# Closing a decode kernel: the waits for the output DMAs move from the gathering of the engines to the reset of the semaphores, and the release of the engines goes

## The chip, the cores and the metric

The kernel runs on one core of one Trainium2 chip. The metric is the device time of one execution in microseconds (us). The profile tells engines apart as PE (matrix engine; PEld is its weight load), DVE (vector), ACT (scalar), POOL (GpSimd) and SP (sync); an engine name with a "q" behind it is that engine's sequencer, whose records below are waits, semaphore updates, drains and DMA issues. The span is the time from the first to the last instruction of the program in the profile; the measured time is longer (383.49 us against a span of 381.7 in before), and the trace records semaphore updates on both sides of the span, which are read here as runtime code.

A semaphore is a counter by which engines and DMAs signal each other; an update is one change of it, recorded in the trace with its time. The landing of a DMA is the last update of its semaphore. A drain is an instruction of the closing block that works on no tensor and can carry a wait or an update; an empty one carries neither. The gather is GpSimd's wait until all other engines have reported, the release its update that lets them go on. A hop is the time from one update of the runtime's barrier to the next.

A ratio given here is the mean time of one kernel's fast runs over that of the other's fast runs of the same rounds, so it is not quite the ratio of the medians quoted beside it. "Before" and "after" are the kernel without and with the change. Each set of experiments had its own runs of before on the same chip, and each time below is set against those.

## The reference, cut to what matters

```python
x = A_x                                             # one token, D = 1024
g = _sigmoid((x * gate_w).sum(-1, keepdims=True))
a = _A_ref(x, A_k_cache, A_v_cache, A_wq, A_wo)     # attention over 65536 cached keys, 4 KV heads of 128
b = _B_ref(x, B_w_in, B_w_sp, B_b_sp, B_w_out)      # a gated MLP
return g * a + (1 - g) * b                          # (1, 1, 1024), bf16
```

For one token, 162 MB of cache and weights are read, and 2 KB of result are written. The change does not touch any of this arithmetic.

## The kernel before

The end of the body, and the function that rewrites the program's closing block when the program is finalized:

```python
out_sb = const.tile([P, NO], BF16, name="out_sb")
nc.scalar.copy(out=out_sb[:], in_=out_ps[:])
for i, queue in enumerate((nc.scalar, nc.sync)):        # two output DMAs, from ACT and from SP
    p0 = (2 * i + 1) * B - 1
    ins = queue.dma_start(out=out_rows[2 * i:2 * i + 2, :], in_=out_sb[p0:p0 + 2, :])
    out_queues.append(ins.ins.name)
...
def close_with_one_barrier(n):
    block = n.main_func.blocks[-1]
    ...
        if engine == mybir.EngineType.Pool:
            assert kinds == ["InstDrain", "InstEventSemaphore", "InstEventSemaphore",
                             "InstDrain", "InstISA", "InstDrain", "InstEventSemaphore",
                             "InstEventSemaphore"]
            drop += [l[2][0], l[6][0]]
            closer = l[0][0]
            continue
        ...
        assert kinds == ["InstDrain", "InstEventSemaphore"] * 2
        drop += [l[1][0], l[2][0]]
    ...
    waits.sort(key=lambda w: w.id in final)             # the two output DMAs last
    block.instructions[closer] = copy.replace(
        block.instructions[closer], sync_info=mybir.SyncInfo(on_wait=waits, on_update=[]))
```

What remains in the closing block of before:

- PE, DVE, ACT and SP: a drain that adds 1 to the gather semaphore (number 96), then a wait for the release semaphore (97).
- GpSimd: waits for all loads and engines and, last, for the two output DMAs (semaphore 102 for the one from ACT, 103 for the one from SP); a drain; the gather (wait until 96 is 4); the reset drain; the clear of semaphores 99 to 110; a drain; the release (97 += 4).

Behind the last instruction of that block the trace of before still records nine updates of semaphore 2, which no instruction of the kernel names, one update each of 248 other semaphores (382.365 to 383.019 us), and nine more updates of semaphore 2. They are read here as closing code of the runtime: a barrier of all engines, a reset of the semaphores, and a second barrier.

## Time and profile before

| what | value | where it is read |
|---|---|---|
| time | 383.56 us median of 6 runs (383.31 to 383.75) | results |
| time and span of the profiled run | 383.49 and 381.7 us | results, head of the page |
| HBM loads | 98.7% of the span, 16 DMA engines | queues on the page |
| after the last load | 2.70 us with PE 0.28 and ACT 0.37 us busy | windows |
| later output landing to the end of the span | 381.698 - 381.028 = 0.670 us | records of the trace |
| first to last update of the runtime's first closing barrier | 382.456 - 381.937 = 0.519 us | updates of semaphore 2 |

The page of before. The DMA row is the busy share of the DMA engines in tenths, for 40 equal slices of the span; the queue's line has packets, MB and share:

```profile
span 381.7 us, 2586 instructions
...
DMA  9999999999999999999999999999999999999995
...
q1 hardware_dynamic: 4324, 162.01, 98.7%
```

Everything but the last slice is read as bound by the loads, whose packets fill 98.7% of the span. Next, busy time of each engine in two windows of before, with the granted clock, the share of DMA and GB/s at the end of each line:

```profile
345.00:379.00 34.00, 21.20 (x236) 8.66 (x182) 4.29 (x7) 0.00 (x0) 0.00 (x0) 0.80 0.95 402
379.00:381.70 2.70, 0.28 (x4) 0.08 (x3) 0.00 (x0) 0.37 (x1) 0.00 (x0) 1.00 0.00 1
```

In the last 2.70 us nothing is loaded (a DMA share of 0.00, 1 GB/s). The instructions of the closing block (all carry line 557) and the issue of the output DMAs (line 521) of before; columns are line, engine, operation, count, then the shortest, median and longest duration in ns, then the first and last start in us:

```profile
L521 SPq DMA_DIRECT2D out_dram<-out_sb x1: 315/315/315, 379.7 to 379.7; - x1
L521 ACTq DMA_DIRECT2D out_dram<-out_sb x1: 254/254/254, 379.7 to 379.7; - x1
...
L557 POOLq EVENT_SEMAPHORE  x7: 17/43/2600, 373.9 to 381.6; - x7
L557 POOLq DRAIN  x3: 34/41/72, 381.1 to 381.5; - x3
L557 DVEq DRAIN  x1: 343/343/343, 370.6 to 370.6; - x1
L557 PEldq DRAIN  x1: 345/345/345, 379.0 to 379.0; - x1
L557 ACTq DRAIN  x1: 241/241/241, 380.0 to 380.0; - x1
L557 SPq DRAIN  x1: 177/177/177, 380.1 to 380.1; - x1
L557 POOLq EVENT_SEMAPHORE_RANGE_CLEAR  x1: 96/96/96, 381.4 to 381.4; - x1
L557 SPq EVENT_SEMAPHORE  x1: 17/17/17, 381.6 to 381.6; - x1
L557 ACTq EVENT_SEMAPHORE  x1: 17/17/17, 381.6 to 381.6; - x1
L557 DVEq EVENT_SEMAPHORE  x1: 21/21/21, 381.6 to 381.6; - x1
L557 PEldq EVENT_SEMAPHORE  x1: 51/51/51, 381.6 to 381.6; - x1
```

The four engines had drained by about 380.3 us, but all three of GpSimd's drains start at 381.1 us or later: they stand behind the wait for the output DMAs. The same instructions with their full time stamps, and the updates of the semaphores, from the records of the trace of before (us from the span's start, duration in ns in brackets):

```
output DMAs issued     SP 379.721 [315]   ACT 379.725 [254]
landed in full         ACT (102) 380.853   SP (103) 381.028      <- the later one
GpSimd  wait 102+105 380.877 [43] | wait 103+107 381.052 [42] | drain 381.139 [41] | gather 381.224 [17]
        reset drain 381.304 [72] | clear 381.405 [96] | drain 381.530 [34] | release 381.594 [17]
others  take the release: SP 381.635  ACT 381.639  DVE 381.647  PE 381.647 [51], ends 381.698
semaphore 2, barrier just before the kernel: nine updates, -0.375 to -0.004
semaphore 2, first closing barrier:  381.937 381.971 382.172 382.216 382.239 382.337 382.375 382.409 382.456
semaphore 2, second closing barrier: 383.243 to 383.600
```

The start on record of a last wait is the moment it was met, not the moment it began: GpSimd's wait for semaphore 103 starts 24 ns after the landing's update in before (381.052 against 381.028).

### The profile page before, as it was taken

The page shows a single profiled execution, that of the slowest core. Times are in us where ns is not written, and L with a number is a line of the kernel's source. Part 1 is how long each engine was busy: PE and PEld are TensorE (multiplying, and loading weights), DVE is VectorE, ACT ScalarE, POOL GpSimd, SP SyncE. Part 2 cuts the span into 40 slices and gives each one's busy share as a digit, 9 for nine tenths or more (in the row PEclk, how much of TensorE's full clock was granted, in tenths as well). Part 3 has the DMA queues.
Part 4 walks back from the last instruction along what each step waited for, and adds up shares of the span by engine and source line. Part 5 has one row for each costly group of instructions (what it writes and reads, how often), then busy time and mean ns, then how long its engine had stood idle before and what let it go on. Part 6 is the DMA issues. An engine that isn't in the chain of part 4 may idle for free.

```text
span 381.7 us, 2586 instructions
## 1 busy us (share of the span) xinstructions
PE 229.4 (60%) x1372; PEld 56.6 (15%) x796; DVE 218.4 (57%) x211; ACT 39.6 (10%) x55; POOL 4.4 (1%) x10
## 2 busy tenths in 40 slices
PE   0433465678157934796379539762977196749355
PEld 0110011112011200121011101110111011212123
DVE  4241487996689306966996058669860497550040
ACT  1010001111601100114011001140100010500000
POOL 4000000000000000000000000000000000000000
PEclk9996569998669885989598958995889599969768
DMA  9999999999999999999999999999999999999995
GB/s 376 438 419 422 433 435 440 433 471 415 407 426 440 440 441 426 440 433 440 440 428 440 440 440 433 434 427 426 412 433 441 433 440 413 428 419 433 433 414 220
DMA packets 4376, 162.17 MB, mean 425 GB/s; under 512 B 521, under 2 KB 525, under 8 KB 909
## 3 DMA queue, kind: packets, MB, share of 16 engines
q1 hardware_dynamic: 4324, 162.01, 98.7%
q8 instruction: 8, 0.13, 0.1%
q14 instruction: 4, 0.02, 0.0%
q10 hardware_dynamic: 40, 0.01, 0.0%
HBM read 162.01 MB, written 0.00 MB: 424 GB/s over the span
## 4 chain that ended last, share of the span: by engine, by line
DMA 60%; PE 20%; DVE 15%; issue 1%; ACT 1%; SPq 1%; DVEq 0%; ACTq 0%
DMA kv<-in_A_k_cache_dram 38%; PE s_ps L388 15%; DVE kv L381 9%; DMA kv<-in_A_wo_dram 8%; DMA kv<-in_A_wq_dram 7%; DMA kv<-in_A_v_cache_dram 7%; PE o_ps L434 3%; DVE pt L424 2%; DVE mx L383 1%; DVE o_sb L448 1%; PE q_ps L274 1%; ACT sc L421 1%; DVE rowt L444 1%; ACT sc L399 1%; SPq L165 1%
## 5 line engine op out<-in xcount | busy, mean ns | idle before, releaser
L388 PE MATMUL s_ps<-kv,wt 128*128 128x512 bf16 x512 | 138.1, 427 | 85.4 <-DVE kv L381 85.4
L381 DVE STREAM_TRANSPOSE kv<-kv 128x2048 int32<-128x2048 int32 x64 | 142.7, 2280 | 58.8 <-DMA kv<-in_A_k_cache_dram 58.8
L434 PE MATMUL o_ps<-kv,pt 128*64 128x512 bf16 x512 | 62.6, 404 | 7.5 <-DMA kv<-in_A_v_cache_dram 7.5
L388 PEld LDWEIGHTS <-wt 128*128 128x128 bf16 x256 | 27.1, 106 | 197.7 <-issue 133.8
L399 ACT CAST sc<-s_ps 128x1024 bf16<-128x1024 f32 x16 | 16.2, 1013 | 253.0 <-PE s_ps L388 253.0
L434 PEld LDWEIGHTS <-pt 128*64 128x64 bf16 x256 | 16.2, 116 | 51.3 <-issue 48.4
L424 DVE STREAM_TRANSPOSE pt<-sc 128x1024 bf16<-128x1024 bf16 x16 | 18.6, 1217 | 6.8 <-ACT sc L421 6.8
L444 DVE TENSOR_TENSOR rowt<-o_ps,own 128x1024 f32<-128x1024 f32 x4 | 4.8, 1195 | 25.7 <-PE o_ps L434 25.7
L421 ACT ACTIVATE sc<-sc,nb 128x1024 bf16<-128x1024 bf16 x16 | 18.2, 1137 | 12.2 <-DVE nb L417 12.2
L383 DVE TENSOR_REDUCE mx<-sc 128x1 f32<-128x1024 bf16 x12 | 14.5, 1206 | 7.0 <-ACT sc L399 7.0
L454 PE MATMUL om_ps<-o_sb,hsel 128*32 128x128 f32 x8 | 2.5, 421 | 19.7 <-DVE o_sb L448 19.7
L403 DVE TENSOR_REDUCE mx<-sc 128x1 f32<-128x1024 bf16 x4 | 4.9, 1220 | 13.6 <-ACT sc L399 13.6
L274 PE MATMUL q_ps<-kv,xT 128*32 128x512 bf16 x64 | 7.2, 630 | 7.3 <-DMA kv<-in_A_wq_dram 7.3
L274 PE MATMUL z_ps<-kv,xT 128*32 128x448 bf16 x64 | 6.4, 577 | 3.9 <-DMA kv<-in_B_w_in_dram 3.9
L475 PE MATMUL out_ps<-kv,oa 128*32 128x256 bf16 x128 | 6.5, 364 | 3.3 <-DMA kv<-in_A_wo_dram 1.9
L341 DVE TENSOR_TENSOR rowt<-q_ps,own_b 128x512 f32<-128x512 f32 x2 | 1.3, 686 | 12.4 <-PE q_ps L274 12.4
L448 DVE TENSOR_REDUCE o_sb<-rowt 128x128 f32<-128x1024 f32 x4 | 7.5, 1872 | 0.1
L289 DVE TENSOR_TENSOR rowt<-z_ps,own_b 128x448 f32<-128x448 f32 x2 | 1.2, 620 | 8.6 <-PE z_ps L274 8.6
L274 PEld LDWEIGHTS <-xT 128*32 128x32 bf16 x64 | 3.0, 139 | 19.3 <-issue 19.3
L230 PE MATMUL xb_ps<-xg,spread 8*128 8x256 bf16 x1 | 0.4, 367 | 9.0 <-DMA xg<-in_gate_w_dram 9.0
L475 PEld LDWEIGHTS <-oa 128*32 128x32 bf16 x128 | 4.5, 129 | 5.5 <-issue 2.7
L518 ACT CAST out_sb<-out_ps 128x256 bf16<-128x256 f32 x1 | 0.4, 372 | 45.6 <-PE out_ps L475 45.6
(88 smaller groups left out, 54.9 us busy)
## 6 DMA issues: line engine op xcount, KB each, us to landing
kv<-in_A_k_cache_dram SPq DMA_DIRECT2D x4, 4096.0 KB, 26.8
kv<-in_A_wq_dram SPq DMA_DIRECT2D x2, 4096.0 KB, 32.9
kv<-in_A_v_cache_dram SPq DMA_DIRECT2D x2, 4096.0 KB
kv<-in_B_w_in_dram SPq DMA_DIRECT2D x2, 3584.0 KB, 15.1
kv<-in_A_wo_dram SPq DMA_DIRECT2D x1, 4096.0 KB
kv<-in_B_w_out_dram SPq DMA_DIRECT2D x1, 3584.0 KB
kv<-in_A_wo_dram SPq DMA_DIRECT2D x1, 2048.0 KB, 28.1
kv<-in_A_wo_dram SPq DMA_DIRECT2D x1, 1024.0 KB, 30.2
```

The source lines that it names most:

```text
L274: ins = nc.tensor.matmul(ps[t * B:(t + 1) * B, k * HN:k * HN + n], lhsT=xT[:, i * KH + c:i * KH + c + 1].to_broadcast([P, B]), rhs=w[:, c, ...
L381: nc.vector.transpose(out=kb[:, v * n:(v + 1) * n], in_=kb[:, v * n:(v + 1) * n])
L383: nc.vector.reduce_max(**late.pop())
L388: ins = nc.tensor.matmul(s_ps[:, k * HN:(k + 1) * HN], lhsT=wt[g % 2][:, v, b].rearrange("p a v h -> p (a v h)"), rhs=kx[:, b // 2, b % 2, ...
L399: nc.scalar.copy(out=sct[g, j][:], in_=s_ps[:])
L403: nc.vector.reduce_max(**late.pop())
L421: nc.scalar.activation(out=sct[g, j][:], in_=sct[g, j][:], func=ACT.Exp, scale=SCALE, bias=nb[:, 0:1], accum_out=lss[g][:, j:j + 1])
L424: nc.vector.transpose(out=ptt[g, j][:].rearrange("p c x -> p (c x)"), in_=sct[g, j][:])
L434: ins = nc.tensor.matmul(o_ps[g][hs, e, :], lhsT=ptt[g, j][:, 2 * u:2 * u + 2, :].rearrange("p c x -> p (c x)"), rhs=vx[:, 2 * u + e], sta ...
L444: nc.vector.tensor_tensor(out=om8, in0=o_ps[g][:].rearrange("p e (v d) -> p (e v) d", d=DH), in1=own_8[:].unsqueeze(2).to_broadcast([P, 2 ...
L448: nc.vector.tensor_reduce(out=o_sb[:], in_=om8.rearrange("p x d -> p d x"), axis=AX.X, op=ALU.add)
L475: nc.tensor.matmul(out_ps[t * B:(t + 1) * B, :], lhsT=vec[:, c0 + c:c0 + c + 1].to_broadcast([P, B]), rhs=w[:, c, t * NO:(t + 1) * NO], st ...
```

## The change

Its intent: GpSimd can do the drain and the gather while the output DMAs are still under way, and needs their completion only before it resets their semaphores. The other engines have nothing left to do once they have been gathered, so nobody needs to release them. The diff; every changed line is shown, "..." stands for unchanged ones:

```diff
-                drop += [l[2][0], l[6][0]]
-                closer = l[0][0]
+                drop += [l[2][0], l[6][0], l[7][0]]
+                closer, reset = l[0][0], l[3][0]
+                assert not l[3][2].has_wait() and not l[3][2].has_update()
                 continue
...
             assert kinds == ["InstDrain", "InstEventSemaphore"] * 2
-            drop += [l[1][0], l[2][0]]
+            drop += [l[1][0], l[2][0], l[3][0]]
...
-        waits.sort(key=lambda w: w.id in final)
-        block.instructions[closer] = copy.replace(
-            block.instructions[closer], sync_info=mybir.SyncInfo(on_wait=waits, on_update=[]))
+        for at, w in ((closer, [w for w in waits if w.id not in final]),
+                      (reset, [w for w in waits if w.id in final])):
+            block.instructions[at] = copy.replace(
+                block.instructions[at], sync_info=mybir.SyncInfo(on_wait=w, on_update=[]))
```

In the built program, the reset drain itself carries the wait for semaphore 102, and one more instruction ahead of it the wait for 103.

## The prediction

> **What bounds the kernel now.** The body is bound by HBM loads: on the page the DMA row is 9 tenths in all slices but the last, the load queue's packets fill 98.7% of the span, at 425 GB/s. The change touches only the last 2.7 us: in the window from 379.0 to 381.7 us the DMA share is 0.00, PE works 0.28 us and ACT 0.37 us. Everything there is serial and exposed.
>
> The closing instructions and the semaphore updates recorded in the trace give the end of before:
> - 379.695 the cast of the result ends; 379.72 both output DMAs are issued; ACT's has landed at 380.853, SP's at 381.028.
> - All four engines have reported to GpSimd by 380.272: the SP output DMA is the last thing awaited.
> - GpSimd after that: wait on SP's DMA 381.052, drain 381.139, gather 381.224, reset drain 381.304, range clear 381.405, drain 381.530 (34 ns), release 381.594 to 381.611. The four others take the release from 381.635; PE's is the last, 51 ns long, to 381.698.
>
> So 0.67 us lie between the last landing and the end of the span.
>
> **What changes, with costs.** No compute or load instruction moves on any engine.
> 1. The waits on the output DMAs move behind the gather, so the first drain and the gather run before the landing, near 380.3 us. From its wait (381.052) GpSimd goes to the reset drain in one step (about 87 ns): 381.304 - 381.139 = 0.165 us less, all on the critical path.
> 2. The release and the four waits for it go. The span then ends with GpSimd's last drain, which took to 381.564: 381.698 - 381.564 = 0.134 us less.
>
> The span should go from 381.70 to about 381.40 us.
>
> **From span to time.** The measured 383.49 is 1.8 us over the span of that run. In the trace the runtime's closing barrier follows: nine updates of semaphore 2 from 381.937 to 382.456, 0.52 us; the same nine took 0.37 us just before the kernel began and 0.36 us at the second closing barrier. [...] The extra is one hop of 0.201 us (381.971 to 382.172) in place of 0.038: one engine came late. If that is GpSimd, only its own earlier end counts: 381.611 to 381.40, -0.21 us. If it was an engine held by the release, up to about 0.16 us more can be gained. I expect -0.2 to -0.35 us, centre -0.25: 0.07%, below the spread of the three times before (383.31 to 383.65).
>
> **Prediction.** 383.25 us, 8 in 10 between 382.85 and 383.65. Faster by over 2%: 0.005; within 2%: 0.99; slower: 0.005.
>
> **What would show it.** Span about 381.4; gather and first drain of GpSimd near 380.3; reset drain about 0.1 us after the later landing; no instruction of PE, DVE, ACT or SP after about 380.3; the hop of 0.2 us gone or kept, which tells who was late; DMA share and groups unchanged.
>
> **What would make it wrong.** The output DMA's landing (1.3 us after its issue) varies by more than 0.2 us and hides or doubles the gain; the reset drain with a wait costs more than a plain one; the runtime's closing code waits for something later than GpSimd; run-to-run spread of the loads, some tenths, decides the sign of the medians.

0.165 and 0.134 us are read from the trace of before, and so are the hop of 0.201 us and the 0.038 us it is set against. The sums: -0.21 us if GpSimd is late, up to about 0.16 us more if another engine is, centre -0.25.

## The result, and the profile after

After takes 383.23 us (median of 6 runs, 383.11 to 383.30), before 383.56 us (6 runs). The ratio is 0.9992, 95% interval 0.9979 to 1.0005: "the same" at the level of per cents. The profiled runs of both, 383.12 and 383.49 us, are fast. The page and the windows of after:

```profile
span 381.3 us, 2581 instructions
...
q1 hardware_dynamic: 4324, 162.01, 98.8%
```

```profile
345.00:379.00 34.00, 19.33 (x224) 8.26 (x176) 4.29 (x7) 0.00 (x0) 0.00 (x0) 0.81 0.94 399
379.00:381.70 2.70, 0.18 (x4) 0.00 (x0) 0.00 (x0) 0.37 (x1) 0.00 (x0) 0.50 0.00 1
```

The loads are as they were. The fixed windows cut PE's work at slightly different places (236 against 224 matmuls recorded); in all, both pages count 1372 of PE. Five instructions are gone (2586 to 2581: the release and four waits for it). The closing block of after (its line is now 559, the output DMAs' 523), in the columns explained above:

```profile
L523 SPq DMA_DIRECT2D out_dram<-out_sb x1: 330/330/330, 379.6 to 379.6; - x1
L523 ACTq DMA_DIRECT2D out_dram<-out_sb x1: 258/258/258, 379.6 to 379.6; - x1
...
L559 POOLq EVENT_SEMAPHORE  x6: 17/43/10008, 368.8 to 380.9; - x6
L559 POOLq DRAIN  x3: 34/41/72, 379.7 to 381.2; - x3
L559 DVEq DRAIN  x1: 343/343/343, 369.1 to 369.1; - x1
L559 PEldq DRAIN  x1: 457/457/457, 378.8 to 378.8; - x1
L559 ACTq DRAIN  x1: 240/240/240, 379.9 to 379.9; - x1
L559 SPq DRAIN  x1: 164/164/164, 380.0 to 380.0; - x1
L559 POOLq EVENT_SEMAPHORE_RANGE_CLEAR  x1: 96/96/96, 381.1 to 381.1; - x1
```

GpSimd's first drain now starts at 379.7 us, 1.2 us ahead of the landing, and there is no line of SP, ACT, DVE or PE at the end. With full time stamps, from the records of the trace of after:

```
landed in full         ACT (102) 380.749   SP (103) 380.924
GpSimd  drain 379.680 [41] | gather 380.200 [17] | wait 103 380.948 [17]
        reset drain 381.009 [72] | clear 381.110 [96] | drain 381.235 [34], ends 381.269
semaphore 2, first closing barrier:  379.481 380.322 381.793 381.837 381.860 381.958 381.997 382.031 382.078
semaphore 2, second closing barrier: 382.865 to 383.223
```

The two profiled runs differ by 383.49 - 383.12 = 0.370 us. The trace splits that without a remainder:

| part | before | after | difference |
|---|---|---|---|
| span's start to the later landing (body and output DMA) | 381.028 | 380.924 | -0.104 |
| later landing to the third update of the first closing barrier | 1.144 | 0.869 | -0.275 |
| third update to the last update of the second barrier | 1.428 | 1.430 | +0.002 |
| last update to the measured time | -0.110 | -0.103 | +0.007 |
| sum | 383.490 | 383.120 | -0.370 |

The first row is the chance of the body: the cast of the result starts between 379.23 and 379.56 us in the fast profiles, and at 379.23 and 379.44 us in two profiles of one and the same kernel (after, and after again). The second row is the change. From here on that interval, later landing to third update, is what the experiments are judged by; the next section shows why the third.

### The profile page after: what moved, and what is told of

The parts are those of the page before. It is cut to its first block, busy times and chain, and to the rows that moved or that the text cites. A ratio compares the mean times of both kernels' runs of the same rounds, so it can differ in the third digit from the quotient of the medians.

```text
span 381.3 us, 2581 instructions
## 1 busy us (share of the span) xinstructions
PE 226.1 (59%) x1372; PEld 56.1 (15%) x796; DVE 218.5 (57%) x211; ACT 39.6 (10%) x55; POOL 4.4 (1%) x10
## 4 chain that ended last, share of the span: by engine, by line
DMA 60%; DVE 18%; PE 17%; issue 2%; ACT 1%; SPq 1%; DVEq 0%; ACTq 0%
DMA kv<-in_A_k_cache_dram 37%; PE s_ps L390 12%; DVE kv L383 12%; DMA kv<-in_A_wo_dram 9%; DMA kv<-in_A_wq_dram 7%; DMA kv<-in_A_v_cache_dram 7%; PE o_ps L436 3%; DVE pt L426 2%; DVE mx L385 1%; DVE o_sb L450 1%; PE q_ps L276 1%; ACT sc L423 1%; DVE rowt L446 1%; ACT sc L401 1%; SPq L167 1%
## 5 line engine op out<-in xcount | busy, mean ns | idle before, releaser
L436 PE MATMUL o_ps<-kv,pt 128*64 128x512 bf16 x512 | 60.4, 394 | 7.8 <-DMA kv<-in_A_v_cache_dram 7.8
```

Source lines behind the costliest of these rows:

```text
L436: ins = nc.tensor.matmul(o_ps[g][hs, e, :], lhsT=ptt[g, j][:, 2 * u:2 * u + 2, :].rearrange("p c x -> p (c x)"), rhs=vx[:, 2 * u + e], sta ...
```

## The experiments

Theory C: from the later landing on, one chain decides: GpSimd's remaining steps, then GpSimd's arrival in the runtime's barrier, then the barrier. Each step taken off GpSimd behind the landing counts in full; what the other engines do counts for nothing. Rival R: the engines that the release held back are what the barrier waits for, and freeing them is the gain. Rival D: the medians differ by drift of the loads. The kernels of all experiments gave the correct result.

### e1_late_wait: the first half alone

```diff
  (against after)
-                drop += [l[2][0], l[6][0], l[7][0]]
+                drop += [l[2][0], l[6][0]]
-            drop += [l[1][0], l[2][0], l[3][0]]
+            drop += [l[1][0], l[2][0]]
```

> Only the first half of the change: the output-DMA waits stand behind the gather, the release and the four waits for it stay. Theory C (chain through GpSimd): the drain and the gather leave the path after the later landing, so from that landing to the third update of the runtime's barrier it takes about 1.144 - 0.165 - 0.026 = 0.95 us (before 1.144, after 0.869); span about 0.19 us under before, time about 383.35 us. Theory R (rival: the other engines, held by the release, are what the runtime's barrier waits for, and freeing them is the gain): time stays within 0.05 us of before and the closing hop of 0.2 us stays because PE is still released last; landing to third update above 1.1 us. Theory D (rival: the medians differ by drift of the loads): any time, no relation to the closing.

Measured: 383.33 us (5 runs, 383.20 to 383.36) against 383.46 us for before (9 runs); ratio 0.9996, 0.9982 to 1.0010. Later landing (381.056) to third update (382.008): 0.952 us, 0.192 under before. The hop of 0.2 us is still there (381.807 to 382.008). Span end minus landing: 381.534 - 381.056 = 0.478 us, 0.192 under before's 0.670. So the first half gives 0.192 us by itself, with the release in place. The closing lines of e1:

```profile
L559 POOLq DRAIN  x3: 34/41/72, 379.8 to 381.4; - x3
...
L559 PEldq EVENT_SEMAPHORE  x1: 51/51/51, 381.5 to 381.5; - x1
```

GpSimd's first drain has moved ahead of the landing, and PE still takes the release last.

### e2_no_release and e2b_no_release: the second half alone

```diff
  (against before)
-                drop += [l[2][0], l[6][0]]
+                drop += [l[2][0], l[6][0], l[7][0]]
-            drop += [l[1][0], l[2][0]]
+            drop += [l[1][0], l[2][0], l[3][0]]
```

> Only the second half: the release and its four waits go, the output-DMA waits stay ahead of the gather. Theory C: the span falls by about 0.13 us (it ends with GpSimd's last drain), but the time only by what GpSimd itself saves, 0.05 to 0.08 us: landing to third update 1.06 to 1.10 us; time about 383.5 us. Theory R: the time falls by most of the whole gain, 0.2 us or more, with landing to third update near 0.9 us.

> e2_no_release again, whose profiled run fell in a slow execution, for a profile in the fast state. Theory C: span ends with GpSimd's last drain, landing to third update 1.06 us as in the slow profile; time 0.05 to 0.1 us under before. Theory R: 0.2 us or more under before.

The first attempt's profiled execution: slow (391.15 us, clock 0.691); its four fast runs were 383.33 to 383.63 us, median 383.41, before 383.46; ratio of the fast runs 1.0000, 0.9986 to 1.0014. The repeat: 383.37 us (4 runs, 383.31 to 383.41) against 383.51 (9 runs of before); ratio 0.9997, 0.9983 to 1.0010. Later landing (381.032) to third update (382.093): 1.061 us, 0.083 under before. The span ends 381.568 - 381.032 = 0.536 us after the landing, 0.134 under before. Its lines:

```profile
L557 POOLq DRAIN  x3: 34/41/72, 381.1 to 381.5; - x3
...
L557 PEldq DRAIN  x1: 347/347/347, 379.0 to 379.0; - x1
```

Of the span's 0.134 us only 0.083 are gained up to the third update: GpSimd ends 0.047 us sooner after the landing (0.536 against 0.583 us), and its update follows 0.525 us after that end and not 0.561. The medians are 0.14 us apart where 0.05 to 0.1 was expected; both lie within the spread of the runs. PE is done at 379.3 us here and yet the third update comes only 0.083 us sooner relative to the landing: this contradicts R, which asked for most of the gain. And 0.192 + 0.083 = 0.275 us, which is what the whole change gives (1.144 - 0.869). The halves add. The intervals of before and of e1 come from one profile each; that of after came out the same in its second profile (after again), and the slow profile of e2 has the same 1.061 us as its repeat. D falls with this as well: these intervals begin behind the last load and contain none of it.

### e3_gpsimd_drains and e4_others_drains: who is waited for

Sixteen empty drains are put behind the last drain of GpSimd (e3), or behind the gather drains of the four others (e4). One more changed line, not shown, keeps the name of GpSimd's last drain as `last_drain`:

```diff
  (against after; the condition is for e3, for e4 it is x.engine != mybir.EngineType.Pool)
+        more = []
+        for i, x in enumerate(block.instructions):
+            if (type(x).__name__ == "InstDrain" and x.name == last_drain):
+                more.append((i, x))
+        for i, x in reversed(more):
+            for k in range(16):
+                block.instructions.insert(i + 1, copy.replace(
+                    x, name=f"I-{900000 + 100 * i + k}",
+                    sync_info=mybir.SyncInfo(on_wait=[], on_update=[])))
```

> The changed kernel with 16 more empty drains on GpSimd after its last one, about 64 ns a step by the trace of before (381.530 to 381.594), about 1.0 us in all. Theory C: span, landing to third update and time all grow by about 1.0 us (third update 1.9 us after the landing, time 384.25 us): GpSimd is what the runtime's barrier waits for. Theory R: the time stays at about 383.25 us.

> The changed kernel with 16 more empty drains on each of PE, ACT, DVE and SP after its report to GpSimd, about 1.0 us on each. Theory C: they end near 381.2 us, before GpSimd comes to the runtime's barrier (381.8), so the time stays at 383.23 +- 0.1 us and landing to third update at 0.87 us. Theory R: the time grows by several tenths to 1 us.

The 1.0 us of both texts is an estimate: 16 steps of the 64 ns that GpSimd took from its last drain to the release in before. For the other engines the text of e4 gives no source of its own.

e3 measured 384.20 us (4 runs, 384.17 to 384.23) against 383.46 for before; ratio 1.0019, 1.0006 to 1.0033. Later landing to third update is 1.843 us, 0.974 more than after; the drains step by 0.061 us, and 16 of them are 0.976. Its lines of GpSimd:

```profile
L568 POOLq DRAIN  x19: 34/34/72, 379.8 to 382.4; - x19
...
L568 POOLq EVENT_SEMAPHORE_RANGE_CLEAR  x1: 96/96/96, 381.3 to 381.3; - x1
```

The first two updates (379.625 and 380.466) did not wait for them; the third and all behind it did. The third update is GpSimd's, and it comes 0.524 us after GpSimd's last instruction, as in after.

In e4, later landing to third update stayed at 0.870 us, though SP ended at 381.206 and PE at 380.587. The time, however, was 383.41 us (4 runs, 383.26 to 383.42) against 383.46 for before, outside the 383.23 +- 0.1 that was expected. Both barriers come as early as in after (last update 2.295 us after the landing, after 2.299), yet the measured time lies 0.031 us above the last update where it lies 0.10 to 0.11 below it in the other profiles so far. Two more runs followed that up.

### e4b_pe_drains and e4c_three_drains: which engines carry e4's extra time

```diff
  (against e4: the condition)
-            if (type(x).__name__ == "InstDrain" and x.engine != mybir.EngineType.Pool):
+            if (type(x).__name__ == "InstDrain" and x.engine == mybir.EngineType.PE):    # e4b
+            if (type(x).__name__ == "InstDrain" and x.engine not in (                    # e4c
+                    mybir.EngineType.Pool, mybir.EngineType.PE)):
```

> In e4 the landing to third update was 0.870 us as in the changed kernel, yet the measured time lies 0.03 us above the last update of semaphore 2 instead of 0.10 to 0.11 us below it, and 1.96 to 2.02 us above the span instead of 1.8 to 1.9. Here the 16 drains stand on PE alone. If PE's longer stream makes that 0.13 us, time minus span is about 2.0 us here; if not, 1.8 to 1.9 us and the time is that of the changed kernel.

> The same with the 16 drains on ACT, DVE and SP, none on PE: the complement of e4b. Time minus span about 2.0 us here if one of these three makes the 0.13 us, 1.8 to 1.9 us if PE does. Landing to third update 0.87 us in both.

| | e4b (PE) | e4c (ACT, DVE, SP) |
|---|---|---|
| time, before beside it | 383.14, 383.43 us | 383.32, 383.43 us |
| ratio | 0.9991 (0.9974 to 1.0008) | 0.9999 (0.9984 to 1.0014) |
| later landing to third update | 0.870 us | 0.869 us |
| measured time minus last update | -0.113 us | +0.031 us |
| time minus span, all four runs (spans on record to 0.1 us) | 1.82 to 1.84 us | 1.97 to 1.98 us |

```profile
L568 PEldq DRAIN  x17: 8/8/460, 378.9 to 380.5; - x17
```

```profile
L569 DVEq DRAIN  x17: 10/10/345, 369.3 to 370.3; - x17
L569 ACTq DRAIN  x17: 8/8/240, 380.0 to 380.9; - x17
L569 SPq DRAIN  x17: 7/7/165, 380.1 to 381.1; - x17
```

The lines are the drains of e4b and then of e4c. In e4b PE worked 1.2 us longer for nothing (later landing to third update 0.870 us, after 0.869). The first update moves with it (379.481 in after, 380.729 in e4b, 0.192 us after PE's end), so the first update is PE's. The second is pushed along, one hop behind it (380.763); the third stays where it was, 0.870 us after the landing. In e4c the second moves to 380.976, 0.112 us after ACT's end, while DVE ended at 370.35: the second is ACT's. The 0.14 us come with the longer streams of ACT, DVE or SP and lie outside the chain of updates. Which of the three it is, and what they are, stays open. For the change it means: with no such drains on them, the others add nothing that shows (measured time minus last update -0.103 us in after, -0.110 in before); that an engine may be given more work for nothing is shown for PE alone, and for 1.2 us.

### a2_after_again and e5_swap: one more step off the chain

In all fast profiles the DMA from ACT lands 0.174 or 0.175 us before the one from SP. After waits for the later one first and then needs another instruction for the earlier one. e5 turns the order around:

```diff
  (against after)
-                      (reset, [w for w in waits if w.id in final])):
+                      (reset, [w for w in waits if w.id in final][::-1])):
```

> The changed kernel again, so that the others of this call have it beside them on the same chip. Theory C: later landing to third update of the runtime's barrier 0.87 us, as before (0.869); time 0.2 to 0.35 us under before.

> The changed kernel with the two output waits swapped: the wait for the ACT DMA, which lands 0.175 us earlier in every trace so far, on the event-semaphore instruction, the wait for the SP DMA on the reset drain itself. Theory C: one step (0.061 us, 380.948 to 381.009 in the trace of after) leaves the path; landing to third update 0.81 us, time 0.06 us under the changed kernel. If the step after a wait were a fixed delay of the landing's news, it stays at 0.87 us.

After again: 383.19 us (5 runs, 383.14 to 383.37) against 383.51 for before (9 runs); ratio 0.9993, 0.9981 to 1.0006; later landing to third update 0.869 us, the same to the nanosecond. e5: later landing (381.084) to third update (381.892) 0.808 us, 0.061 less, as expected: the reset drain starts 24 ns after the landing. The time, 383.22 us (5 runs, 383.17 to 383.27), does not show it; half of the 0.061 us is gone again by the last update of the second barrier (2.269 us after the landing, against 2.300), and the rest is below the spread. As a gain in time, e5 is inconclusive.

### e7_sp_closes: another engine closes

With GpSimd shown to be the engine waited for, and 0.524 us from its last instruction to its update, the closing was given to SP: GpSimd only reports, SP gathers, waits and clears.

```diff
  (against after)
+        swap = {mybir.EngineType.Pool: mybir.EngineType.SP,
+                mybir.EngineType.SP: mybir.EngineType.Pool}
+        for i, x in enumerate(block.instructions):
+            if x.engine in swap:
+                block.instructions[i] = copy.replace(x, engine=swap[x.engine])
```

> The changed kernel with SP and GpSimd exchanged in the closing: SP gathers, waits for the output DMAs and clears the semaphores; GpSimd only reports. Theory C with a cost of GpSimd's own (it needs 0.52 us from its last instruction to its update of the runtime's barrier, PE 0.19 to 0.24 and ACT 0.11 to 0.15): landing to the fifth update, 1.211 us before and 0.936 after, falls to 0.45 to 0.60 us, the 0.2 us hop moves from the third to the fifth update, and the time is 0.3 to 0.45 us under the changed kernel. Rival P: the 0.52 us belong to whichever engine closes last; then landing to fifth update is about 0.87 us and the time is at most 0.1 us under the changed kernel.

Measured: 382.59 us (5 runs, 382.53 to 382.83) against 383.51 for before (ratio 0.9977, 0.9963 to 0.9990) and 383.19 for after: 0.60 us less, where 0.3 to 0.45 was expected. The late update is now the fifth (380.741, then 381.603), which is therefore SP's. The lines of e7 (the closing block's line is 564):

```profile
L564 SPq EVENT_SEMAPHORE  x6: 17/28/28, 380.3 to 381.3; - x6
L564 SPq DRAIN  x3: 7/7/7, 380.6 to 381.5; - x3
L564 POOLq DRAIN  x1: 4106/4106/4106, 1.0 to 1.0; - x1
...
L564 SPq EVENT_SEMAPHORE_RANGE_CLEAR  x1: 52/52/52, 381.4 to 381.4; - x1
```

GpSimd is done 5.1 us into the kernel. Later landing (381.261) to fifth update is 0.342 us, after had 0.936: 0.594 us less, below the 0.45 to 0.60 expected. SP's own steps take 0.218 us from the landing to its end (GpSimd's 0.345): a drain is 7 ns long and not 34 to 72, the clear 52 and not 96. From its end to its update SP needs 0.124 us where GpSimd needed 0.524, and two more hops to the fifth. So 0.345 - 0.218 = 0.127 us come from quicker steps and 0.524 + 0.067 - 0.124 = 0.467 from the arrival. Why GpSimd needs so long from its last instruction to its update was not tested. Rival P, by which the 0.52 us belong to whichever engine closes last, has fallen.

### e8_sp_swap and e7b_sp_closes: both together

e8 is e7 with the swapped waits of e5.

> SP closes and, in addition, the wait for the DMA that lands last stands on the reset drain. Theory C: both savings add: one SP step (381.335 - 381.278 = 0.057 us) leaves the path of e7, so later landing to fifth update 0.342 - 0.057 = 0.285 us, time about 0.06 us under e7 beside it, about 0.95 us under before. If the two do not add, it stays at 0.34 us.

> e7 again beside e8. Theory C: landing to fifth update 0.34 us again, SP's last instruction to its update 0.12 us again, time about 0.9 us under before (382.6 us).

e8: 382.54 us (5 runs, 382.46 to 382.74) against 383.49 for before (9 runs); ratio 0.9975, 0.9963 to 0.9988. Later landing (381.069) to fifth update (381.354) is 0.285 us, as expected. e7 again: 382.68 us (5 runs, 382.56 to 382.79), ratio 0.9977, 0.9964 to 0.9991, and 0.342 us to the fifth update, as the first time. e8 is the fastest version found, 0.95 us under before, by the medians; that it beats e7 is shown by the interval in the trace (0.057 us), while the times (0.14 us apart) overlap.

```profile
L564 SPq EVENT_SEMAPHORE  x6: 17/28/28, 380.1 to 380.9; - x6
L564 SPq DRAIN  x3: 7/7/7, 380.4 to 381.2; - x3
```

In e8 the last wait on an event-semaphore instruction starts at 380.9 us, at the earlier landing, and the later one is met on the drain.

### All intervals side by side

```
                    later landing to   3rd update   5th update   time (us)   before beside it
before                                 1.144        1.211        383.56
e1  late wait only                     0.952        1.020        383.33      383.46
e2b no release only                    1.061        1.128        383.37      383.51
after                                  0.869        0.936        383.23      383.56
after again                            0.869        0.936        383.19      383.51
e3  16 drains on GpSimd                1.843        1.910        384.20      383.46
e4  16 drains on the four others       0.870        0.937        383.41      383.46
e4b 16 drains on PE                    0.870        0.937        383.14      383.43
e4c 16 drains on ACT, DVE, SP          0.869        0.936        383.32      383.43
e5  swapped waits                      0.808        0.875        383.22      383.51
e7  SP closes                                       0.342        382.59      383.51
e7b SP closes, again                                0.342        382.68      383.49
e8  SP closes, swapped waits                        0.285        382.54      383.49
```

## Why the prediction was right

- **Size.** Predicted 383.25 us, measured 383.23. By the medians before and after are 0.33 us apart, and 0.32 in the repeat; the prediction's centre was 0.25. The chain in the trace gives 0.275 up to the third update and 0.273 up to the last. The rest of the medians' difference is not shown to be the change's: the six runs of before alone spread over 0.44 us (383.31 to 383.75). The 95% intervals of the ratio contain 1, so by time alone the sign is not settled, though all six runs of after lie below all six of before. That 383.25 was hit to 0.02 us is partly luck: it took 0.25 off the 383.50 of before's first three runs, where later the medians gave 0.33 off 383.56, and the two differences nearly cancel. The range named (382.85 to 383.65) is wide enough to hold the 383.56 of before itself, so the time alone tests nothing; the steps below were tested. By the trace the sign is settled, since both halves and their sum come out to the nanosecond.
- **Step 1, the waits move, -0.165 us.** Right in kind, short by 0.027: e1 shows 0.192 us. Nearly all of the missing part, 0.026 us, is the last wait. In before that event-semaphore instruction carried two waits and was 42 ns long, with 87 ns to the next instruction; in after it carries one and is 17 ns long, with 61 ns to the next. The prediction had taken over the 87 ns.
- **Step 2, the release goes, -0.134 us of span.** Right to the nanosecond: e2b, 0.134 us.
- **From span to time.** The prediction left open whether GpSimd or an engine held by the release was the late one, with -0.21 us for the first case. It was GpSimd (e3, e2b, e7). The 0.21 (0.212 unrounded, 381.611 to 381.399) was too small by 0.063 us, for two reasons: the 0.026 us of the last wait, and that GpSimd's update comes 0.561 us after its last instruction when that is the release, but 0.524 us when it is the drain, 0.037 less. The centre that was named, -0.25, lay between the two cases and so came close to 0.275 by being hedged, not by a better sum. "Everything there is serial and exposed" was too broad: of the release's 0.134 us, 0.083 counted.
- **Signs named beforehand.** The span went to 381.27 us where 381.40 was expected; 0.104 us of that is the body's chance. The gather was at 380.200 us, as expected; the first drain was at 379.680, well before the 380.3 expected, because nothing in front of it waits for the output DMAs any more. The reset drain came 0.085 us after the later landing (expected about 0.1). No instruction of the other engines came after 380.174 us. The hop of 0.2 us was kept, and grew to 1.471 us (380.322 to 381.793), since PE and ACT now arrive earlier and GpSimd is still the one awaited.
- **Feared and not seen.** The output DMA's landing hardly varies: from 1.293 to 1.308 us after its issue on SP in all 14 profiles. The reset drain with a wait on it took 72 ns, as without one.

## What to carry to other kernels

In this kernel, once the last output DMA had landed, what stood behind that landing on the engine that closes counted up to the barrier's third update (16 drains on GpSimd added 0.974 us, e3), and 16 drains on each of the others did not (0.001 us, e4), though the measured time of e4 lay 0.13 to 0.14 us further above its last update, for a reason left open. So move waits for outputs as far back as their semaphores' reset allows (0.192 us here, e1), let that last wait be on the DMA that lands last, and put it on the instruction that needs it (the last two steps gave 0.057 to 0.061 us in the trace, e5 and e8, and were not visible in the times). The end of the span was not the end of the time here: freeing the engines that nobody waited for shortened the span by 0.134 us and the interval to the third update by 0.083 (e2b). Before polishing the steps of the closing engine, ask which engine should close: giving it to SP in place of GpSimd gained 0.59 us up to the fifth update, twice what this change gave, and 0.60 us by the medians.

## What else the traces show

- The runtime's barrier: its nine updates took 0.371 us before the kernel and 0.357 at the second closing barrier of before; no single hop of the two took more than 0.112 us. The order in which the engines come in the first closing barrier: the first update is PE's (e4b), the second ACT's (e4c), the third GpSimd's (e3), the fifth SP's (e7), so the fourth is left for DVE, if each engine makes one of the first five.
- How long each engine takes from its last instruction to its update: GpSimd 0.524 us behind a drain (0.561 behind the release), SP 0.124 us (e7), ACT 0.112 us behind empty drains (e4c) and 0.157 behind its gather drain (after: 380.165 to 380.322), PE likewise 0.192 (e4b: 380.537 to 380.729) and 0.244 us (after: 379.237 to 379.481). The difference between GpSimd and SP decided e7.
- The reset of the semaphores at the end: in before its recorded updates run from 382.365 to 383.019, 0.654 us, and from the last update of the first closing barrier to the first of the second it is 0.787 us in all (382.456 to 383.243).
- An event-semaphore instruction with two waits does not always start when both are met: on GpSimd such instructions are 42 or 43 ns long at the least where one with a single wait is 17, and in after the one for semaphores 104 and 101 is 10.008 us long: it starts at 368.755, ahead of the landing on 101 at 378.733, so part of its waiting lies inside its window.
- Empty drains in the kernel's closing, by engine: their median was 7 ns on SP, 8 on ACT and PE, 10 on DVE (e4b, e4c) and 34 on GpSimd, where each stepped the chain by 61 ns (e3).
